# Performer attention and a channel mixer on one core: batch 2's DRAM copies moved ahead of the channel weights, the second weights moved behind its transposes, tails of q and k loaded as fp16, k evacuated by ScalarE

## The chip, the cores and the metric

The kernel runs on one core of a Trainium2 chip. The metric is device microseconds of one execution. Engines are named as in the profile: PE (matrix multiplies; PEld its weight loads), DVE (VectorE), ACT (ScalarE), POOL (GpSimd) and SP (SyncE, here only a queue that issues DMAs).

## The reference

Eight batches of eight heads, 576 positions, head size 64. Attention with random features, then a mixer over tokens and channels:

```
proj = x @ omega.T ; phi(x) = exp(proj - |x|^2/2 - max) / sqrt(128)      # x = q or k, scaled by 64 ** -0.25
kv   = phi(k).T @ v ; z = sum(phi(k)) ; x = (phi(q) @ kv) / (phi(q) @ z + 1e-6)
x    = heads side by side: [8, 576, 512]
u    = x + (relu(x.T @ w_tok1) @ w_tok2).T          # tokens: 576 -> 256 -> 576
out  = u + relu(u @ w_ch1) @ w_ch2                  # channels: 512 -> 1536 -> 512
```

Factors that are common to a row of q cancel in the division, so the kernel needs only exponentials of the projections and a maximum for k.

## The kernel before, in words

Each sequence of 576 is split into a main part of 512 and a tail of 64. For each batch the kernel needs q and k with the head size on the partitions (`qT`, `kT`), since the projection with `omega` contracts over it. There are two ways to them.

Batches 0 and 1 (the start): main parts are loaded through the GpSimd software DMA queue, which casts to fp16 on the way (`load_nat`), and PE transposes them (`t_main`, L255) into PSUM; DVE copies the result out (L258). The first two heads of batch 0 come as fp32 through SP's and ACT's queues and are cast by DVE (`stage_qk`, `cast_qk`). Tails come as fp32 through SP's and ACT's queues (`stage_tail`, L131), are cast by DVE (L265), transposed by PE (L268) and copied out by DVE (L269).

Batches 2 to 7: `cast_dram` (L80) copies q and k as fp16 into DRAM through the software queue, and `load_T` (L88) loads them with DMA transposes issued on SP's queue. The main part and the tail lie together in that copy. `load_T_v` also issues the loads of v (L106) and of v's tail (L115) on SP, behind the transposes.

Per batch, then: `q_tail` (L278) and `k_tail` (L289: a copy of k's tail columns; L293) project the tails; for each pair of heads `q_proj` (L327) and `k_proj` (L339) with exponentials on ACT (L272); `k_max` takes k's maximum on DVE (L351, L355, L359) and multiplies v by its reciprocal (L360; on DVE for batch 0, on POOL after); `kv` (L372, L377) and ACT's copy (L385); `num` (L396), `norm` (L404, L405), `num_tail` (L418, L427, L428). The tail's maximum and multiplies are `k_tail_max` (L305 to L315). Token mixing is `tok1` (L441, L444), `tok2` (L457, L460) and a transpose on PE (L480, L481); channel mixing is `ch1` (L495, relu on ACT L502) and `ch2` (L507, add on DVE L516, store L518). `ch1` reads the first channel weights `wc1` (loaded in two halves, L228), `ch2` the second, `wc2` (two halves, L234); in the profile both are named `wc`.

The order on every engine is written by hand: each step gets a place, one unit per pair of heads (batch b begins at 4b), from a table of offsets (`L`, `O`, `O1`), and the steps are issued sorted by place. An engine works through its instructions in that order; a DMA on POOL or SP is one of them, so a DMA that has to wait holds what stands behind it. The software queue has eight completion slots in turn: a DMA on POOL also waits until the one issued eight before it has landed.

Of the kernel before, what the change touches and what calls it, by code (L numbers as in the profile page):

```python
# [9 lines left out]
FP32 = mybir.dt.float32  # L10
FP16 = mybir.dt.float16
# [6 lines left out]
def kernel(  # L18
# [17 lines left out]
    nc = tc.nc  # L36

    B, H, S, D = q.shape
# [5 lines left out]
    SM = 512  # L44
    ST = S - SM
# [8 lines left out]
    ldpool = ctx.enter_context(tc.tile_pool(name="ld", bufs=3))  # L54
# [7 lines left out]
    def att_ps(shape, dt, name):  # L62
        return pspool.tile(shape, dt, name=name, tag="attps", bufs=3)
# [8 lines left out]
    SP2 = S // 2  # L72
    NP2 = SM // 2
    live = {}
# [18 lines left out]
    def load_v(b):  # L93

        if b < 2:
            t = ldpool.tile([P, H, NJ, D], FP16, name="v_16", tag="v_16", bufs=2)
            live["v", b] = t
            nc.gpsimd.dma_start(
                out=t.rearrange("p h j d -> p h (j d)"),
                in_=v[b, :, 0:SM, :].rearrange("h (p j) d -> p h (j d)", j=NJ),  # L100
            )
# [18 lines left out]
    stage = {}  # L120
# [4 lines left out]
        eng.dma_start(out=t, in_=src[0, 0:2, 0:SM, :].rearrange("h (p j) d -> p h (j d)", j=NJ))  # L125
        stage[which] = t

    def stage_tail(eng, b, which):
        src = q if which == "q" else k
        t = ldpool.tile([ST // 2, H, 2 * D], FP32, name=f"stt_{which}", tag="stt", bufs=2)  # L130
        eng.dma_start(out=t, in_=src[b, :, SM:S, :].rearrange("h (c w) d -> c h (w d)", w=2))  # L131
        stage[which, b] = t

    def new_nat(b):
        for which in "qk":
# [20 lines left out]
    stage_qk(nc.scalar, "k")  # L156
    om_f = wpool.tile([P, D], FP32, name="om_f")
    nc.sync.dma_start(out=om_f, in_=omega)
    stage_tail(nc.scalar, 0, "k")
    stage_tail(nc.sync, 0, "q")  # L160
    ident16 = wpool.tile([P, P], FP16, name="ident16")
    make_identity(nc, ident16)
    load_nat(0, 2, 4, "q")
    load_nat(0, 2, 4, "k")
    load_nat(0, 4, 8, "q")
    load_nat(0, 4, 8, "k")
    load_v(0)
    load_v_tail(0)

# [14 lines left out]
    wc1 = wpool.tile([P, ND, DC], FP16, name="wc1")  # L184
    wc2 = wpool.tile([P, NCB, DM], FP16, name="wc2")
# [40 lines left out]
    def load_wc1(part):  # L226
        c0, c1 = part * DC // 2, (part + 1) * DC // 2
        nc.gpsimd.dma_start(  # L228
            out=wc1[:, :, c0:c1], in_=moe_w_ch1[:, c0:c1].rearrange("(i p) c -> p i c", p=P)
        )  # L230
# [11 lines left out]
    def at(place, fn, *args):  # L242
        steps.append((place, len(steps), fn, args))


    def t_main(b, h0, n, which):

        if h0 == 0:
            live[which + "T", b] = ldpool.tile(
                [P, H, SP2], FP16, name=f"{which}T", tag=f"{which}T", bufs=2  # L250
            )
        ps = att_ps([P, n, 2, P], FP16, "t_ps")
        for i in range(n):
            for e in range(2):
                nc.tensor.transpose(  # L255
                    ps[:, i, e, :], live[which + "nat", b][:, h0 + i, e * P : (e + 1) * P], ident16
                )
        nc.vector.tensor_copy(  # L258
            out=live[which + "T", b][:, h0 : h0 + n, 0:NP2],
            in_=ps.rearrange("r h e p -> r h (e p)"),  # L260
        )

    def t_tail(b, which):
        nt = ldpool.tile([ST // 2, H, 2 * D], FP16, name="natt", tag="natt", bufs=1)
        nc.vector.tensor_copy(out=nt, in_=stage[which, b])  # L265
        ps = att_ps([P, H, ST // 2], FP16, "tt_ps")
        for h in range(H):
            nc.tensor.transpose(ps[:, h, :], nt[:, h, :], ident16[0 : ST // 2, 0 : ST // 2])  # L268
        nc.vector.tensor_copy(out=live[which + "T", b][:, :, NP2:SP2], in_=ps)  # L269

    def exp(out, in_):
        nc.scalar.activation(out=out, in_=in_, func=AF.Exp, bias=0.0, scale=c_scale)  # L272
# [13 lines left out]
    def k_tail(b):  # L286
        sb = live["kT", b]
        kt = apool.tile([P, H, ST // 2], FP16, name="k_tt", tag="k_tt")
        nc.vector.tensor_copy(out=kt, in_=sb[:, :, NP2:SP2])  # L289
        live["kpt", b] = apool.tile([P, 4, M], FP16, name="k_pt", tag="k_pt")  # L290
        ps = att_ps([P, 4, M], FP32, "kt_ps")
        for g in range(2):
            nc.tensor.matmul(  # L293
                ps[:, 2 * g : 2 * g + 2, :],
                kt[:, 4 * g : 4 * g + 4, :].rearrange("r h c -> r (h c)"),
                bd,
                start=True,
                stop=True,
            )
        exp(live["kpt", b], ps)  # L300
# [222 lines left out]
            nc.sync.dma_start(out=out[2 * j + 1, SM:S, :], in_=o[ST:P])  # L523


    L = {"dram2": 2.516, "wc2": 2.862, "tq": -0.681, "tk": -0.669, "tail": 0.285, "dram": 2.006, "T": 2.8, "klo": 1.094, "khi": 3.57, "clo": 4.0}
    O = {"qt": -0.334, "kt": 0.536, "ktm": 1.279, "q0": 0.018, "q1": 0.449, "k0": 0.06, "k1": 0.182, "km": 0.711, "kv": 1.426, "num": 1.72, "dn": 0.204, "norm": 1.74, "nt": 2.248}
    O1 = {"qt": 2.914, "kt": 0.685, "ktm": 1.13}
    def load_second():
        load_wtok()  # L530
        load_nat(1, 0, 4, "q")
        load_nat(1, 0, 4, "k")
        load_nat(1, 4, 8, "q")
        load_nat(1, 4, 8, "k")
        load_v(1)
        stage_tail(nc.sync, 1, "q")
        stage_tail(nc.sync, 1, "k")
        load_v_tail(1)
        load_wc1(0)
        load_wc1(1)  # L540

    at(-0.97, cast_qk, "q")
    at(-0.96, cast_qk, "k")
    at(-0.90, load_second)
    at(L["dram2"], cast_dram, 2, "q")
    at(L["dram2"], cast_dram, 2, "k")
    at(L["wc2"], load_wc2, 0)
    at(L["wc2"], load_wc2, 1)
    at(0.05, clear_vz)
    at(0.95, clear)  # L550
    at(2.95, permute_w2)
    for b in range(2):
        n = 2 if b == 0 else 4
        for h0 in range(0, H, n):
            at(4 * b + h0 / 2 + L["tq"], t_main, b, h0, n, "q")
            at(4 * b + h0 / 2 + L["tk"], t_main, b, h0, n, "k")
        at(4 * b + L["tail"], t_tail, b, "k")
        at(4 * b + L["tail"] + 0.001, t_tail, b, "q")

    def load_T_v(b):  # L560
        for which in "qk":
# [8 lines left out]
        at(4 * (b - 2) + L["T"], load_T_v, b)  # L570

    for b in range(B):
        o = dict(O)
        if b < 2:
            o.update(O1)
# [24 lines left out]

    for b in range(B):
        items = [(5, tok1, b, 0), (5, tok1, b, 1), (2, tok2, b, 0), (2, tok2, b, 1)]
        items += [(1, tokT, b, 0), (2, tok2, b, 2), (1, tokT, b, 1), (2, tok2, b, 3)]
        if b % 2:
            items += [(4, tok2_tail, b // 2)]
        items += [(1, tokT, b, 2), (1, tokT, b, 3)]
        if b % 2:
            items += [(1, u_transpose, ut[b // 2], uTt[:, :, b // 2, :])]
        spread(4 * (b + 1) + L["klo"], 4 * (b + 1) + L["khi"], items)

    for c in range(B + 1):
        items = [(4, ch1, c, cb) for cb in range(NCB)] + [(12, ch2, c, j) for j in range(NJ)]
        spread(4 * (c + 1) + L["clo"], 4 * (c + 2) + L["clo"], items)

    for _, _, fn, args in sorted(steps, key=lambda s: s[:2]):
        fn(*args)
# [30 lines left out]
```

## Time and profile before

| | us |
|---|---|
| median of 3 runs | 339.85 (339.14 to 340.18) |
| the profiled execution | 338.85 |
| its span, first to last instruction | 336.8 |
| PE busy | 305.8 |
| DVE busy | 180.9 |
| ACT busy | 152.3 |
| POOL busy | 69.0 |

In the profile's rows a number behind an operation's `x` counts instructions; the figure in brackets is the engine's idle time just before the row and what ended it. A DMA's "us to landing" runs from its issue until its data are there. Durations come from the one profiled execution.

### The profile page before, as it was taken

How to read it: one execution, taken by the hardware profiler on the slowest of the kernel's cores; microseconds unless marked ns; L12 is line 12 of the kernel's file. 1: busy time of each engine (PE TensorE's matmuls, PEld its weight loads, DVE VectorE, ACT ScalarE, POOL GpSimd, SP SyncE). 2: the span in 40 equal slices, each digit the busy share in tenths (PEclk: the TensorE clock that was granted, in tenths of full speed). 3: DMA queues.
4: the chain of work that ended last, by engine and by line, in shares of the span. 5: the costliest groups of instructions: out<-in, count | busy, mean ns of one | idle time of the engine just before them, and what ended most of it. 6: DMA issues, size and time to landing. Idle time of an engine off the chain costs nothing.

```text
span 336.8 us, 5538 instructions
## 1 busy us (share of the span) xinstructions
PE 305.8 (91%) x2137; PEld 162.6 (48%) x2137; DVE 180.9 (54%) x479; ACT 152.3 (45%) x293; POOL 69.0 (20%) x92
## 2 busy tenths in 40 slices
PE   5666781699999999999999999999999999999994
PEld 2444540354555555555555555555555544444441
DVE  3898894254855386547754865576548415202011
ACT  1545360385248525842585267426742540250620
POOL 8540341024112411331132124012401100000000
PEclk9657798599999999999999999999999999999999
DMA  9999995998358537772767294001001001102014
GB/s 177 206 201 215 204 196 100 229 183 190 103 104 241 105 99 145 201 140 64 152 194 140 64 220 125 31 33 63 2 31 65 31 2 62 62 2 93 31 31 93
DMA packets 59689, 39.01 MB, mean 116 GB/s; under 512 B 30096, under 2 KB 54544, under 8 KB 59280
## 3 DMA queue, kind: packets, MB, share of 16 engines
q1 hardware_dynamic: 49552, 24.55, 30.1%
q0 software_dynamic: 9568, 13.73, 24.7%
q10 hardware_dynamic: 544, 0.39, 0.4%
q8 instruction: 16, 0.26, 0.3%
q14 instruction: 9, 0.07, 0.1%
HBM read 35.88 MB, written 16.52 MB: 156 GB/s over the span
## 4 chain that ended last, share of the span: by engine, by line
PE 74%; DMA 14%; POOL 4%; DVE 4%; SPq 3%; issue 1%; POOLq 0%
PE h_ps L507 28%; PE h_ps L495 25%; DMA q<-in_q_dram 6%; DMA kT<-k 5%; PE ht_ps L457 4%; PE k_ps L339 3%; DMA w2raw<-in_moe_w_tok_dram 3%; PE q_ps L327 3%; SPq L88 3%; POOL vz L315 2%; PE h_ps L441 2%; PE uT_ps L480 2%; PE num_ps L396 2%; PE kv_ps L372 1%; PE kv_ps L377 1%; PE htt_ps L468 1%
## 5 line engine op out<-in xcount | busy, mean ns | idle before, releaser
L507 PE MATMUL h_ps<-wc,r 128*128 128x512 f16 x432 | 98.1, 379 | 0.0
L495 PE MATMUL h_ps<-uT,wc 128*128 128x512 f16 x384 | 93.9, 382 | 0.0
L502 ACT ACTIVATE r<-h_ps 128x512 f16<-128x512 f32 x108 | 64.6, 598 | 57.7 <-PE h_ps L495 57.3
L507 PEld LDWEIGHTS <-r 128*128 128x128 f16 x432 | 41.1, 98 | 45.1
L272 ACT ACTIVATE q_p<-q_ps 128x512 f16<-128x512 f32 x64 | 38.3, 598 | 49.8 <-PE q_ps L327 49.7
L495 PEld LDWEIGHTS <-wc 128*128 128x128 f16 x432 | 41.0, 98 | 40.4 <-issue 0.8
L360 POOL TENSOR_TENSOR v_sc<-v_nat,v_sc 128x512 f16<-128x512 f32 x24 | 25.4, 1057 | 129.0 <-DVE rc L404 71.2
L516 DVE TENSOR_TENSOR o_sb<-um,h_ps 128x512 f32<-128x512 f16 x32 | 22.0, 688 | 50.7 <-PE h_ps L507 50.4
L272 ACT ACTIVATE k_p<-k_ps 128x512 f16<-128x512 f32 x64 | 36.5, 601 | 1.1 <-PE k_ps L339 1.1
L404 DVE RECIPROCAL rc<-num_ps 128x4 f32<-128x4 f32 x64 | 10.9, 171 | 32.8 <-PE num_ps L396 32.7
L385 ACT CAST kv_sb<-kv_ps 128x130 f16<-128x130 f32 x32 | 8.5, 267 | 44.2 <-PE kv_ps L377 44.2
L405 DVE TENSOR_TENSOR xm<-num_ps,rc 128x256 f16<-128x256 f32 x64 | 27.2, 424 | 2.2
L327 PE MATMUL q_ps<-qT,bd 128*128 128x512 f16 x64 | 26.2, 409 | 1.0 <-DVE qT L258 1.0
L339 PE MATMUL k_ps<-bd,kT 128*128 128x256 f16 x128 | 25.3, 296 | 0.9 <-DMA kT<-k 0.7
L315 POOL TENSOR_TENSOR vz<-v_tail,vz 32x256 f16<-32x256 f32 x28 | 18.6, 663 | 33.5 <-DVE vz L314 21.7
L460 DVE TENSOR_TENSOR um<-xm,ht_ps 128x512 f16<-128x512 f16 x32 | 21.9, 683 | 2.2 <-PE ht_ps L457 1.9
L355 DVE TENSOR_REDUCE km<-mx 128x8 f16<-128x512 f16 x32 | 22.0, 686 | 1.1
L396 PEld LDWEIGHTS <-q_p 128*128 128x128 f16 x256 | 16.6, 102 | 12.3 <-issue 1.8
L457 PE MATMUL ht_ps<-r,w2m 128*128 128x512 f16 x64 | 19.2, 379 | 0.9 <-DVE r L450 0.5
L339 PEld LDWEIGHTS <-kT 128*128 128x128 f16 x128 | 13.0, 105 | 12.3 <-issue 1.4
L351 DVE TENSOR_TENSOR mx<-k_p 128x512 f16<-128x512 f16 x32 | 13.9, 434 | 9.3 <-ACT k_p L272 9.1
L396 PE MATMUL num_ps<-kv_sb,q_p 128*128 128x65 f16 x256 | 18.4, 200 | 0.6 <-ACT kv_sb L385 0.3
(92 smaller groups left out, 278.7 us busy)
## 6 DMA issues: line engine op xcount, KB each, us to landing
out_dram<-o_sb SPq DMA_DIRECT2D x32, 256.0 KB, 2.4
v_nat<-in_v_dram SPq DMA_DIRECT2D x12, 512.0 KB, 5.4
q<-in_q_dram POOLq DMA_DIRECT2D x6, 576.0 KB, 5.5
k<-in_k_dram POOLq DMA_DIRECT2D x6, 576.0 KB, 8.8
wc<-in_moe_w_ch_dram POOLq DMA_DIRECT2D x4, 768.0 KB, 19.9
v_tail<-in_v_dram SPq DMA_DIRECT2D x32, 32.0 KB, 4.9
v<-in_v_dram POOLq DMA_DIRECT2D x2, 512.0 KB, 10.4
out_dram<-o_sb SPq DMA_DIRECT2D x8, 128.0 KB, 2.3
```

The costliest lines, as they stand in the source:

```text
L272: nc.scalar.activation(out=out, in_=in_, func=AF.Exp, bias=0.0, scale=c_scale)
L315: eng.tensor_tensor(out=vs[r, hh, :, 0:D], in0=live["vt", b][r], in1=vs[r, hh, :, D : D + 1].broadcast_to((32, 4, D)), op=ALU.mult,)
L327: nc.tensor.matmul(ps, bd[:, w * M : (w + 1) * M], sb[:, 2 * hp : 2 * hp + 2, 0:NP2], start=True, stop=True)
L339: nc.tensor.matmul(ps[:, 2 * e : 2 * e + 2, :], sb[:, 2 * hp + i, e * P : (e + 1) * P], bd, start=True, stop=True,)
L355: nc.vector.reduce_max(out=mx, in_=tmp, axis=AX.X)
L360: eng.tensor_tensor(out=vs[:, :, 0:D], in0=live["v", b][:, 2 * hp : 2 * hp + 2].rearrange("p h j d -> p (h j) d"), in1=vs[:, :, D : D + 1] ...
L396: nc.tensor.matmul(ps[:, j, :], live["qp", b, hp][:, j % 2, i, j // 2, :], sb, start=True, stop=True)
L405: nc.vector.tensor_tensor(out=live["x", b][:, :, h * D : (h + 1) * D], in0=ps[:, :, 0:D], in1=rc.unsqueeze(2).broadcast_to((P, NJ, D)), op ...
L457: nc.tensor.matmul(ps, w2m[:, tb, j, :], live["r1", b][:, tb, :], start=(tb == 0), stop=(tb == NT - 1))
L495: nc.tensor.matmul(ps, wc1[:, db, cb * P : (cb + 1) * P], uT[:, db].rearrange("p j c -> p (j c)"), start=(db == 0), stop=(db == ND - 1),)
L502: nc.scalar.activation(out=live["r3", c][:, cb, :], in_=ps, func=AF.Relu)
L507: nc.tensor.matmul(ps, live["r3", c][:, cb, j * P : (j + 1) * P], wc2[:, cb, :], start=(cb == 0), stop=(cb == NCB - 1),)
```

## The change

Six edits.

1. `cast_dram` of batch 2 gets place 1.8 (2.516 before), and the loads of the first channel weights, which stood at the end of `load_second` (place -0.90), get place 1.85, behind it.
2. The loads of the second channel weights, place 2.862 before, stand at 8.473, directly behind `k_tail` of batch 2.
3. The tails of q and k of batches 0 and 1 are loaded as fp16 through the software queue (`load_nat_tail`, L131), in three buffers. The casts on DVE and the loads on SP and ACT go.
4. In `t_main`, k's result leaves PSUM through ACT, q's still through DVE (one line, L258 to L259).
5. The copy in `k_tail` goes to POOL from batch 2 on.
6. The table: batches 0 and 1 get tables of their own, in which a few projections move; from batch 2 on k's projections stand later (0.06 to 0.207 and 0.182 to 0.468), `k_tail` earlier (0.536 to 0.472), token mixing earlier (1.094 to 1.017), and the copies into DRAM of batches 3 to 7 later (2.006 to 2.766).

```diff
-    def stage_tail(eng, b, which):
+    def load_nat_tail(b, which):
         src = q if which == "q" else k
-        t = ldpool.tile([ST // 2, H, 2 * D], FP32, name=f"stt_{which}", tag="stt", bufs=2)
-        eng.dma_start(out=t, in_=src[b, :, SM:S, :].rearrange("h (c w) d -> c h (w d)", w=2))
-        stage[which, b] = t
+        t = ldpool.tile([ST // 2, H, 2 * D], FP16, name="natt", tag="natt", bufs=3)
+        nc.gpsimd.dma_start(out=t, in_=src[b, :, SM:S, :].rearrange("h (c w) d -> c h (w d)", w=2))
+        live[which + "natt", b] = t
...
-        nc.vector.tensor_copy(
+        copy = nc.vector.tensor_copy if which == "q" else nc.scalar.copy
+        copy(
             out=live[which + "T", b][:, h0 : h0 + n, 0:NP2],
...
-        nt = ldpool.tile([ST // 2, H, 2 * D], FP16, name="natt", tag="natt", bufs=1)
-        nc.vector.tensor_copy(out=nt, in_=stage[which, b])
+        nt = live[which + "natt", b]
...
-        nc.vector.tensor_copy(out=kt, in_=sb[:, :, NP2:SP2])
+        (nc.vector if b < 2 else nc.gpsimd).tensor_copy(out=kt, in_=sb[:, :, NP2:SP2])
...
-    at(L["wc2"], load_wc2, 0)
-    at(L["wc2"], load_wc2, 1)
+    at(L["wc1"], load_wc1, 0)
+    at(L["wc1"], load_wc1, 1)
+    for part in range(2):
+        at(8 + O["kt"] + L["wc2"], load_wc2, part)
```

What this does to the order on POOL between batch 1's loads and the second weights, before (`q_374` and `k_376` are batch 2's copies in DRAM, `q_698` and `k_700` batch 3's, `wc_129` the first and `wc_130` the second channel weights, `v_sc` the multiplies of batch 1's v):

```order
L98 DMA v_155<-in_v_dram 128x8x256
L228 DMA wc_129<-in_moe_w_ch_dram 128x4x768 x2
L80 DMA q_374<-in_q_dram 32x9216
L80 DMA k_376<-in_k_dram 32x9216
L234 DMA wc_130<-in_moe_w_ch_dram 128x6x512 x2
L360 TENSOR_TENSOR v_sc<-v_155,v_sc 128x8x64
L315 TENSOR_TENSOR vz_139<-v_tail,vz_139 32x4x64 x4
L360 TENSOR_TENSOR v_sc<-v_155,v_sc 128x8x64
L80 DMA q_698<-in_q_dram 32x9216
L80 DMA k_700<-in_k_dram 32x9216
L360 TENSOR_TENSOR v_sc<-v_155,v_sc 128x8x64 x2
```

And now, at the same place (`q_324` and `k_326` batch 2's, `q_752` and `k_754` batch 3's copies; `natt` a tail of batch 1):

```order
L131 DMA natt<-in_k_dram 32x8x128
L131 DMA natt<-in_q_dram 32x8x128
L98 DMA v_159<-in_v_dram 128x8x256
L80 DMA q_324<-in_q_dram 32x9216
L80 DMA k_326<-in_k_dram 32x9216
L228 DMA wc_129<-in_moe_w_ch_dram 128x4x768 x2
...
L80 DMA q_752<-in_q_dram 32x9216
L80 DMA k_754<-in_k_dram 32x9216
L360 TENSOR_TENSOR v_sc<-v_159,v_sc 128x8x64
L289 COPY k_tt<-kT 128x256
L234 DMA wc_130<-in_moe_w_ch_dram 128x6x512 x2
```

Batch 2's copies have passed the first weights; the second weights stand behind batch 1's last multiply and behind the copy of k's tail columns, which reads the transposed k of batch 2. Batch 3's copies stand behind one more multiply than before.

On DVE, the end of batch 1's first pair of heads and the tails of batch 1, as a difference:

```order
-L265 CAST natt<-stt_k 32x1024
 L269 COPY kT<-tt_ps 128x8x32
-L265 CAST natt<-stt_q 32x1024
 L269 COPY qT<-tt_ps 128x8x32
 L289 COPY k_tt<-kT 128x256
```

Both casts are gone, and the two copies out of PSUM follow each other.

More of the change, by code (lines that the diff above doesn't have):

```diff
@@ L158 @@
     nc.sync.dma_start(out=om_f, in_=omega)
-    stage_tail(nc.scalar, 0, "k")
-    stage_tail(nc.sync, 0, "q")
     ident16 = wpool.tile([P, P], FP16, name="ident16")
@@ L166 @@
     load_nat(0, 4, 8, "k")
+    load_nat_tail(0, "k")
+    load_nat_tail(0, "q")
     load_v(0)
@@ L523, in ch2 @@
             nc.sync.dma_start(out=out[2 * j + 1, SM:S, :], in_=o[ST:P])
-    L = {"dram2": 2.516, "wc2": 2.862, "tq": -0.681, "tk": -0.669, "tail": 0.285, "dram": 2.006, "T": 2.8, "klo": 1.094, "khi": 3.57, "clo": 4.0}
-    O = {"qt": -0.334, "kt": 0.536, "ktm": 1.279, "q0": 0.018, "q1": 0.449, "k0": 0.06, "k1": 0.182, "km": 0.711, "kv": 1.426, "num": 1.72, "dn": 0.204, "norm": 1.74, "nt": 2.248}
-    O1 = {"qt": 2.914, "kt": 0.685, "ktm": 1.13}
+    L = {"dram2": 1.8, "wc2": 0.001, "dram": 2.766, "T": 2.8, "klo": 1.017, "khi": 3.57, "clo": 4.0, "klo0": 1.094, "khi0": 3.57, "clo0": 4.0, "wc1": 1.85}
+    O = {"qt": -0.334, "kt": 0.472, "ktm": 1.279, "q0": 0.018, "q1": 0.449, "k0": 0.207, "k1": 0.468, "km": 0.711, "kv": 1.426, "num": 1.72, "dn": 0.204, "norm": 1.74, "nt": 2.248}
+    O0 = {"qt": 2.914, "kt": 0.685, "ktm": 1.13, "q0": 0.018, "q1": 0.525, "k0": -0.372, "k1": 0.182, "km": 0.711, "kv": 1.426, "num": 1.72, "dn": 0.204, "norm": 1.74, "nt": 2.248, "tq": -0.681, "tk": -0.669, "tail": 0.327}
+    O1 = {"qt": 2.914, "kt": 0.685, "ktm": 1.13, "q0": -0.375, "q1": 0.613, "k0": 0.06, "k1": 0.182, "km": 0.711, "kv": 1.426, "num": 1.72, "dn": 0.219, "norm": 1.74, "nt": 2.248, "tq": -0.681, "tk": -0.669, "tail": 0.285}
     def load_second():
@@ L534, in load_second @@
         load_nat(1, 4, 8, "k")
+        load_nat_tail(1, "k")
+        load_nat_tail(1, "q")
         load_v(1)
-        stage_tail(nc.sync, 1, "q")
-        stage_tail(nc.sync, 1, "k")
         load_v_tail(1)
-        load_wc1(0)
-        load_wc1(1)
     at(-0.97, cast_qk, "q")
@@ L553 @@
         n = 2 if b == 0 else 4
+        o = (O0, O1)[b]
         for h0 in range(0, H, n):
[L555 to L558, printed above, removed]
+            at(4 * b + h0 / 2 + o["tq"], t_main, b, h0, n, "q")
+            at(4 * b + h0 / 2 + o["tk"], t_main, b, h0, n, "k")
+        at(4 * b + o["tail"], t_tail, b, "k")
+        at(4 * b + o["tail"] + 0.001, t_tail, b, "q")
     def load_T_v(b):
@@ L572 @@
     for b in range(B):
-        o = dict(O)
-        if b < 2:
-            o.update(O1)
+        o = (O0, O1)[b] if b < 2 else O
         g = 4 * b
@@ L608 @@
             items += [(1, u_transpose, ut[b // 2], uTt[:, :, b // 2, :])]
-        spread(4 * (b + 1) + L["klo"], 4 * (b + 1) + L["khi"], items)
+        klo, khi = (L["klo0"], L["khi0"]) if b == 0 else (L["klo"], L["khi"])
+        spread(4 * (b + 1) + klo, 4 * (b + 1) + khi, items)
     for c in range(B + 1):
         items = [(4, ch1, c, cb) for cb in range(NCB)] + [(12, ch2, c, j) for j in range(NJ)]
-        spread(4 * (c + 1) + L["clo"], 4 * (c + 2) + L["clo"], items)
+        spread(4 * (c + 1) + L["clo0" if c == 0 else "clo"], 4 * (c + 2) + L["clo"], items)
     for _, _, fn, args in sorted(steps, key=lambda s: s[:2]):
```

## The prediction

> **What bounds the kernel now.** I read the page first, then busy time by stage (windows cut where the matmul stream changes character), then the timeline at the hole this shows, then the queues behind the hole. From the page the clock granted to TensorE in 40 slices, and the stages (start:end, length, then busy us and instruction count of PE, PEld, DVE, ACT, POOL, the clock, DMA share, GB/s):
>
> ```profile
> PEclk9657798599999999999999999999999999999999
> ...
> 8.00:26.80 18.80, 13.35 (x106) 8.23 (x106) 16.66 (x50) 9.41 (x19) 8.88 (x12) 0.60 1.36 203
> 26.80:52.30 25.50, 19.02 (x205) 12.68 (x203) 22.53 (x64) 12.18 (x26) 6.86 (x9) 0.90 1.25 191
> 52.30:61.20 8.90, 0.00 (x0) 0.00 (x0) 2.27 (x6) 0.09 (x1) 1.05 (x1) 0.71 0.77 117
> ...
> 81.90:300.00 218.10, 216.86 (x1537) 115.28 (x1535) 122.03 (x315) 107.21 (x209) 39.45 (x48) 1.00 0.40 98
> ```
>
> Three regimes. From 81.9 to 300 us PE is busy 216.86 of 218.10 us: this stretch can't shrink by more than about 1 us, it can only start earlier. From 8 to 52.3 us DVE is the fullest engine (16.66 of 18.8, 22.53 of 25.5) while PE has holes. From 52.3 to 61.2 us PE does nothing. The timeline says why (start, length, engine, line; in brackets the idle time before it and what ended it):
>
> ```profile
> 51.86 0.40 PE L480 MATMUL uT_ps<-ident,um 128*128 128x128 f16 x4
> 61.23 0.61 PE L278 MATMUL qt_ps<-qT,bd 128*128 128x256 f16 x2 [8.97 <-DMA qT<-q]
> ...
> 68.39 0.38 PE L293 MATMUL kt_ps<-bd,k_tt 128*128 128x256 f16 x2
> ...
> 81.86 1.46 PE L507 MATMUL h_ps<-wc,r 128*128 128x512 f16 x6
> ```
>
> Batch 2's first matmul waits 8.97 us for the DMA transpose of its q. GpSimd's timeline shows in which order the software queue was fed, and single answers on DMA issues give each landing after its issue:
>
> ```profile
> 14.57 0.89 POOL L98 DMA_DIRECT2D v<-in_v_dram  x1 [0.52 <-DMA w1m<-in_moe_w_tok_dram]
> 16.69 1.50 POOL L228 DMA_DIRECT2D wc<-in_moe_w_ch_dram  x2 [1.23 <-DMA w2raw<-in_moe_w_tok_dram]
> 18.17 0.54 POOL L80 DMA_DIRECT2D q<-in_q_dram  x1
> 19.29 0.51 POOL L80 DMA_DIRECT2D k<-in_k_dram  x1 [0.58 <-DMA q_nat<-in_q_dram]
> 20.64 0.87 POOL L234 DMA_DIRECT2D wc<-in_moe_w_ch_dram  x1 [0.84 <-DMA k_nat<-in_k_dram]
> 21.97 0.83 POOL L234 DMA_DIRECT2D wc<-in_moe_w_ch_dram  x1 [0.46 <-DMA q_nat<-in_q_dram]
> 46.09 0.52 POOL L80 DMA_DIRECT2D k<-in_k_dram  x1
> 49.06 1.05 POOL L360 TENSOR_TENSOR v_sc<-v,v_sc 128x512 f16<-128x512 f16 x1 [2.45 <-PE k_ps L339]
> 54.92 1.05 POOL L360 TENSOR_TENSOR v_sc<-v,v_sc 128x512 f16<-128x512 f16 x1 [4.81 <-DVE v_sc L359]
> ```
> ```profile
> v<-in_v_dram POOLq DMA_DIRECT2D x1, 512.0 KB, 12.3
> wc<-in_moe_w_ch_dram POOLq DMA_DIRECT2D x1, 768.0 KB, 16.6
> q<-in_q_dram POOLq DMA_DIRECT2D x1, 576.0 KB, 18.6
> k<-in_k_dram POOLq DMA_DIRECT2D x1, 576.0 KB, 20.2
> wc<-in_moe_w_ch_dram POOLq DMA_DIRECT2D x1, 768.0 KB, 27.7
> k<-in_k_dram POOLq DMA_DIRECT2D x1, 576.0 KB, 15.2
> ```
>
> Issue plus landing: batch 1's v at 26.9, the second half of the first weights at 34.0 (issued half way through the pair, 17.4), q's copy at 36.8, k's at 39.5, the second weights at 49.7, batch 3's copies at 61.3. They land in the order of issue, one after the other. The transposes start only when q's copy is there, and SP's DMA queue shows how long they take beside the rest, against batch 4's:
>
> ```profile
> 36.80 9.21 SPq L88 DMA_TRANSPOSE qT<-q  x1
> ...
> 95.05 2.44 SPq L88 DMA_TRANSPOSE qT<-q  x1
> 97.58 3.16 SPq L88 DMA_TRANSPOSE kT<-k  x1
> ```
> ```profile
> 46.11 17.22 DMA kT<-k
> ```
> ```profile
> kT<-k SPq DMA_TRANSPOSE x1, 6.8
> ```
>
> Batch 2's pair takes from 36.8 to 63.3, 26.5 us; batch 4's, with the queue empty, from 95.05 to 104.4, 9.3 us.
>
> **The change, part by part.**
>
> *Copies ahead of the first weights.* The two weight loads stood for 34.0 - 26.9 = 7.1 us in front of q's copy. The four fp16 tails (64 KB each) join the same queue: at the weights' own rate (2 x 768 KB in 7.1 us) 1.2 us. So q's copy lands at 36.8 - 7.1 + 1.2 = 30.9. For the transposes, the work that shared the engines before was: rest of k's copy 2.7, second weights 10.2, batch 3's copies 11.6, transposes 9.3; 33.8 us of work done in 26.5, a ratio of 0.78. Now: 2.7 + 7.1 (first weights, now behind) + 9.3 = 19.1, times 0.78 is 14.9, so kT lands at about 45.8. The ends are 30.9 + 9.3 = 40.2 (undisturbed) and 30.9 + 26.5 = 57.4 (as slow as before). I take 45.8, because batch 3's copies, which came last before, are issued behind one more GpSimd multiply, the one at 49.06; 4 us earlier (next step) that one ends at 46.1, after the transposes.
>
> *When PE gets there.* DVE sets the pace before the hole, so what leaves DVE counts. The DVE groups between 8 and 52 us, two casts' aftermath, and the first max of batch 0:
>
> ```profile
> L258 DVE COPY kT<-t_ps 128x512 f16<-128x512 f16 x4 | 1.7, 417 | 0.0
> L258 DVE COPY kT<-t_ps 128x1024 f16<-128x1024 f16 x2 | 1.4, 677 | 0.0
> L265 DVE CAST natt<-stt_q 32x1024 f16<-32x1024 f32 x2 | 1.3, 672 | 0.0
> L265 DVE CAST natt<-stt_k 32x1024 f16<-32x1024 f32 x2 | 1.3, 644 | 0.0
> ```
> ```profile
> 13.29 0.42 DVE L351 TENSOR_TENSOR mx<-k_p 128x512 f16<-128x512 f16 x1
> ...
> 34.87 0.29 DVE L269 COPY kT<-tt_ps 128x256 f16<-128x256 f16 x1 [0.45 <-PE tt_ps L268]
> 36.23 0.29 DVE L269 COPY qT<-tt_ps 128x256 f16<-128x256 f16 x1 [0.49 <-PE tt_ps L268]
> ```
>
> 5.7 us of DVE work go away. In batch 1: two k copies 1.36, two casts 1.32, and the round trips 0.45 + 0.49 in which DVE waited for PE between them; 3.6 us. In batch 0 the tails now come through the software queue, fifth and sixth in it; DVE then waits for them in order instead of casting, so the casts and the first two k copies buy nothing there, as the first max comes at about 13.3 either way; the other two k copies give 0.8. Together 4.4; I take 4.0, since PE is at 0.60 of its clock in batch 0 and close behind. Ends: 1.5 (tails land late) and 5.7. ScalarE takes the k copies beside 12.18 of 25.5 busy us, at no cost; were it full, each would cost about the 0.42 or 0.68 us that it took on DVE. The Trainium skill, "DMA: Bandwidth & Descriptors", Specifications, speaks against this part: under 512 B per transfer the engines read, modify and write, and the fp16 tail rows are 256 B. By it (an estimate, at double price) the tails take 2.4 us instead of 1.2, batch 0 starts 1.2 us later and the result is 326.2; no run before shows such rows in this queue.
>
> PE then reaches batch 2 at 52.3 - 4.0 = 48.3, after kT (45.8). The wait of 9.0 us goes and the arrival moves by 4.0.
>
> *The clock.* Behind the hole the clock was low:
>
> ```profile
> 61.20:66.50 5.30, 4.60 (x21) 2.27 (x22) 1.35 (x5) 2.56 (x5) 0.00 (x0) 0.52 1.09 278
> ```
>
> 5.3 us at 0.52 would be 2.8 at full clock: 2.5 us saved if no hole is left. The Trainium skill, "TensorE: Matmul & The Clock Gate", Part 1, has the clock back after about 3.4 us of work; by it 1.7 us would be saved and the time would be 325.8. Here it stayed low for 5.3 us, so I keep 2.5.
>
> *Second weights held.* They stand behind the new copy of k's tail on GpSimd, which waits for kT; queued behind it are the weights and the multiplies for batch 2. The last multiply of batch 1 moves from 54.92 to 50.9 and ends at 52.0; the copy takes at most such a multiply's 1.05, I take 0.5; kt's matmul wants it at 48.3 + (68.39 - 61.23) - 2.5 = 53.0, so nothing is lost there. The first half is issued at 52.5 and takes 0.87 us to issue (row at 20.64), so the second stands at 53.4. The first use, L507, comes 81.86 - 61.23 - 2.5 = 18.1 us after PE's arrival, at 66.4. The shortest landing of such a half is this row's, the longest the 27.7 above:
>
> ```profile
> wc<-in_moe_w_ch_dram POOLq DMA_DIRECT2D x1, 768.0 KB, 13.6
> ```
>
> That gives 67.0 to 81.1, a wait of 0.6 to 14.7 us (0 if it is quicker). I take 0.6: the 27.7 had four transfers in front of it, now only what is left of batch 3's copies.
>
> *The rest.* The fourth tail buffer waits until PE has transposed batch 0's k tail; v, both copies and the weights queue behind it, but PE should be done with it at about 13 (the max at 13.3 stands behind it on DVE), and GpSimd comes there at about 14 (v's issue in the row at 14.57). DVE loses the six later tail copies; it isn't the bound after 61 us. k's projections stand later among the channel matmuls from batch 2 on; with 1.2 us of PE idle in 218, I put this at 0, within 1 us either way.
>
> **The sum**: 9.0 + 4.0 + 2.5 - 0.6 = 14.9. The profiled execution took 338.85 us (span 336.8), so 323.95; the median of the runs shown, 339.85, is 1.0 higher: 325.0.
>
> **The rivals.**
>
> *The transposes still collide.* If the first weights and batch 3's copies hold them back as before, PE waits until 57.4: 9.1 us and the clock's 2.5 come back, 3.3 remain, 336.6. For it: 26.5 against 9.3 us in the rows. Against: one competitor less. By the Trainium skill, "DMA: Bandwidth & Descriptors", Queues, rings and completion order, each DMA engine alternates between queues by packet, so that transposes beside weights crawl until these are through; that speaks for it.
>
> *Second weights late, transposes in time.* A landing half way between 13.6 and 27.7 is 7 us later: 332.
>
> *Slower.* Place: L507 behind the copy of k's tail. If kT lands at 57.4, the second half is issued at 57.4 + 0.5 + 0.87 = 58.8 and at 27.7 lands at 86.5, while PE wants it at 57.4 + 20.6 = 78.0: 8.5 us of wait against 3.9 gained (the collision's 3.3 and the 0.6 counted there), 344.5. It decides from a landing of 23 us on. Against: what fills the queue now stands in front, not behind.
>
> *Nothing of it*: GpSimd already waits for old transfers before each issue, so an earlier place need not land earlier; then 339.85. Against: landing follows issue order in every row.
>
> **Chances.** Forecast 0.66, collision 0.14, late weights 0.12, slower 0.05, nothing 0.03. About 0.3% can be told from no change here. So faster 0.92, same 0.03, slower 0.05. The forecast's own range is 322 to 329 (start gain 1.5 to 5.7, reordering 1). For 8 in 10 it reaches to 333, which takes in the late weights and the milder collisions, and down to 320.5.
>
> **What would show it.** Right: q's copy landing near 31, kT near 46, no DMA wait before PE's third L278 pair near 48, clock 1.0 there, L507 first near 67. Wrong: a wait for qT or kT of over 2 us, tails that hold batch 0 past 14 us, or L507 waiting for wc.

## The result, and the profile after

| | us | ratio to before |
|---|---|---|
| before, median of 4 runs beside it | 340.01 (339.14 to 342.24) | |
| changed kernel, median of 4 runs | 320.73 (320.09 to 321.38) | 0.9424 [0.9373, 0.9474] |
| its profiled execution | 321.38 | |
| its span | 318.9 (before 336.8) | |

The kernel became 19 us faster; the forecast was 325.0. Times and ratios of the experiments below leave disturbed runs out, and the profiles of two of them (the casts back on DVE, the clearing first) fell into such runs and are not read.

The page's row of granted clocks, in 40 slices, no longer has the gap behind the start:

```profile
PEclk9598999999999999999999999999999999999998
```

The stages of the changed kernel (start:end, length, then busy us and count of PE, PEld, DVE, ACT, POOL, the clock, DMA share, GB/s):

```profile
8.00:26.80 18.80, 12.26 (x115) 7.94 (x116) 14.62 (x45) 11.60 (x23) 8.79 (x14) 0.73 1.42 202
26.80:47.00 20.20, 16.11 (x197) 10.32 (x195) 19.05 (x59) 13.07 (x27) 6.72 (x9) 1.00 1.11 207
47.00:52.30 5.30, 5.13 (x44) 2.95 (x42) 3.30 (x10) 4.54 (x10) 2.62 (x4) 1.00 1.16 255
...
65.00:280.00 215.00, 214.44 (x1528) 114.50 (x1527) 120.53 (x310) 105.72 (x207) 41.22 (x55) 1.00 0.49 110
```

Batch 1 is over at 47.0 and not at 52.3, at full clock where it had 0.90; PE then goes on without a pause. DVE is still the fullest engine up to there (19.05 of 20.2 us), as it was before. PE's timeline at the place where the hole was, and at the first use of the second weights:

```profile
46.62 0.40 PE L480 MATMUL uT_ps<-ident,um 128*128 128x128 f16 x4 [0.32 <-DVE um L460]
47.07 0.38 PE L278 MATMUL qt_ps<-qT,bd 128*128 128x256 f16 x2
65.19 2.75 PE L507 MATMUL h_ps<-wc,r 128*128 128x512 f16 x12
```

No bracket stands behind L278 or L507: neither waits. SP's queue, and DMA issues with their time to landing:

```profile
29.69 8.44 SPq L88 DMA_TRANSPOSE qT<-q  x1
38.23 4.94 SPq L88 DMA_TRANSPOSE kT<-k  x1
```
```profile
q<-in_q_dram POOLq DMA_DIRECT2D x1, 576.0 KB, 10.2
kT<-k SPq DMA_TRANSPOSE x1, 7.0
wc<-in_moe_w_ch_dram POOLq DMA_DIRECT2D x1, 768.0 KB, 9.8
wc<-in_moe_w_ch_dram POOLq DMA_DIRECT2D x1, 768.0 KB, 13.9
wc<-in_moe_w_ch_dram POOLq DMA_DIRECT2D x2, 768.0 KB, 11.9
```

GpSimd's queue shows when the second weights are issued:

```profile
50.69 0.39 POOL L289 COPY k_tt<-kT 128x256 f16<-128x256 f16 x1
51.02 1.75 POOL L234 DMA_DIRECT2D wc<-in_moe_w_ch_dram  x2
```

kT has landed at 38.23 + 7.0 = 45.2, 1.9 us before PE wants batch 2. The first half of the second weights lands at 51.02 + 9.8 = 60.8. The second, issued at about 51.9, takes 13.9 and lands at 65.8 (the last row is the mean of the two); the seventh of L507's twelve matmuls, at about 65.19 + 6 x 0.22 = 66.5, is the first that reads it. That is a margin of 0.7 us.

### The profile page after: what moved, and what is told of

It is laid out like the page before. It is cut to its first block, busy times and chain, and to the rows that moved or that the text cites. A ratio compares the mean times of both kernels' runs of the same rounds, so it can differ in the third digit from the quotient of the medians.

```text
span 318.9 us, 5525 instructions
## 1 busy us (share of the span) xinstructions
PE 299.3 (94%) x2137; PEld 159.1 (50%) x2137; DVE 173.8 (55%) x463; ACT 155.8 (49%) x299; POOL 71.6 (22%) x102
## 4 chain that ended last, share of the span: by engine, by line
PE 81%; DVE 10%; DMA 3%; POOL 3%; issue 1%; ACT 0%; POOLq 0%; DVEq 0%
PE h_ps L507 29%; PE h_ps L495 28%; PE ht_ps L457 4%; PE k_ps L339 3%; PE q_ps L327 3%; PE h_ps L441 3%; DMA v<-in_v_dram 3%; PE uT_ps L480 2%; PE num_ps L396 2%; PE kv_ps L372 2%; DVE xm L405 1%; PE kv_ps L377 1%; DVE km L355 1%; PE htt_ps L468 1%; POOL vz L315 1%
## 5 line engine op out<-in xcount | busy, mean ns | idle before, releaser
L507 PE MATMUL h_ps<-wc,r 128*128 128x512 f16 x432 | 98.1, 379 | 0.0
L507 PEld LDWEIGHTS <-r 128*128 128x128 f16 x432 | 41.0, 98 | 45.8
L516 DVE TENSOR_TENSOR o_sb<-um,h_ps 128x512 f32<-128x512 f16 x32 | 22.0, 688 | 48.0 <-PE h_ps L507 47.6
L272 ACT ACTIVATE k_p<-k_ps 128x512 f16<-128x512 f32 x64 | 37.8, 598 | 2.8 <-PE k_ps L339 1.5
L351 DVE TENSOR_TENSOR mx<-k_p 128x512 f16<-128x512 f16 x32 | 13.6, 425 | 37.0 <-ACT k_p L272 37.0
L327 PE MATMUL q_ps<-qT,bd 128*128 128x512 f16 x64 | 24.9, 395 | 1.6 <-DVE qT L259 1.6
L315 POOL TENSOR_TENSOR vz<-v_tail,vz 32x256 f16<-32x256 f32 x28 | 17.3, 616 | 17.0 <-DVE vz L314 15.4
L396 PE MATMUL num_ps<-kv_sb,q_p 128*128 128x65 f16 x256 | 17.9, 195 | 0.1
L339 PEld LDWEIGHTS <-kT 128*128 128x128 f16 x128 | 12.1, 100 | 10.6 <-ACT kT L259 1.7
L441 PE MATMUL h_ps<-xm,w1m 128*128 128x512 f16 x64 | 16.4, 379 | 0.0
## 6 DMA issues: line engine op xcount, KB each, us to landing
wc<-in_moe_w_ch_dram POOLq DMA_DIRECT2D x4, 768.0 KB, 14.9
```

What stands on the lines that cost most here:

```text
L327: nc.tensor.matmul(ps, bd[:, w * M : (w + 1) * M], sb[:, 2 * hp : 2 * hp + 2, 0:NP2], start=True, stop=True)
L339: nc.tensor.matmul(ps[:, 2 * e : 2 * e + 2, :], sb[:, 2 * hp + i, e * P : (e + 1) * P], bd, start=True, stop=True,)
L396: nc.tensor.matmul(ps[:, j, :], live["qp", b, hp][:, j % 2, i, j // 2, :], sb, start=True, stop=True)
L441: nc.tensor.matmul(ps, w1m[:, j, tb * P : (tb + 1) * P], live["x", b][:, j, :], start=(j == 0), stop=False)
L507: nc.tensor.matmul(ps, live["r3", c][:, cb, j * P : (j + 1) * P], wc2[:, cb, :], start=(cb == 0), stop=(cb == NCB - 1),)
```

## The experiments

Twelve kernels ran, in three groups. The theories: that the place of batch 2's copies in the queue made the hole go, as the prediction's working had it; or that it is the traffic behind them, whatever their place. The start's 5.2 us and the 1.2 us gained later have terms of their own. The letters in the expectations change their meaning: in the first group A and B are what each expectation says of them (in the second of its runs B, not A, is the view that the place alone made the hole go); in the second group B is the view that the place decides and C that the traffic does.

### The place of batch 2's copies, alone and undone

The kernel before, with nothing but batch 2's copies ahead of the first weights:

```diff
-        load_wc1(0)
-        load_wc1(1)
...
-    L = {"dram2": 2.516, ...
+    L = {"dram2": 1.8, ...
+    at(1.85, load_wc1, 0)
+    at(1.85, load_wc1, 1)
```

> The kernel before with one edit alone: batch 2's copies ahead of the first weights; the second weights follow directly, and all else is as before. Theory A: q's copy lands at about 29.7 instead of 36.8, but first and second weights (17.3 us of queue) and then batch 3's copies (issued at 45.5) run beside the transposes; with the ratio of 0.78 kT lands at about 52.6, when PE comes (52.3): the 9 us hole and 2.5 us of clock go, 328 to 330 us. Rival B (what stands behind the copies slows the transposes as much as what stood in front): kT lands at 58 to 62 and the time stays at 336 to 340 us.

Measured: 337.74 (335.98 to 339.38, 10 runs), ratio 0.9938 [0.9908, 0.9968]. SP's queue, the landing of its second transpose, and PE at batch 2:

```profile
29.82 10.40 SPq L88 DMA_TRANSPOSE qT<-q  x1
40.32 21.52 SPq L88 DMA_TRANSPOSE kT<-k  x1
```
```profile
kT<-k SPq DMA_TRANSPOSE x1, 23.6
```
```profile
62.07 0.61 PE L278 MATMUL qt_ps<-qT,bd 128*128 128x256 f16 x2 [9.57 <-DMA qT<-q]
```

The transposes start at 29.8, 7 us earlier than before, and kT lands at 40.32 + 23.6 = 63.9, where it landed before (63.3). Going first brings kT no earlier when the first weights, the second and batch 3's copies come behind; where the 0.6% of time comes from was not taken apart. Rival B came, with a landing 1.9 us beyond its range. The other way round, the changed kernel with the first weights ahead of the copies again:

```diff
-"wc1": 1.85}
+"wc1": 1.75}
```

> The changed kernel with one edit taken back: the first channel weights are issued ahead of batch 2's copies again; the second weights stay held. Theory A (the queue lands in order, and only the order of issue matters): q's copy lands 7 to 10 us later than the changed kernel's 29.7, at 37 to 39.5, kT 9.3 to 12 us after that, at 46 to 51, and PE, which is ready at 47.1, waits 0 to 4 us: 321 to 325 us. Rival B (this order alone removed the 9 us hole): the hole comes back, 330 us or more, with the clock low behind it.

Measured: 320.02 (319.83 to 321.16, 4 runs), ratio 0.9434 [0.9398, 0.9469], the changed kernel's own time.

```profile
36.89 3.91 SPq L88 DMA_TRANSPOSE qT<-q  x1
40.96 2.40 SPq L88 DMA_TRANSPOSE kT<-k  x1
```
```profile
kT<-k SPq DMA_TRANSPOSE x1, 4.6
```

The pair starts 7 us later and is through at 40.96 + 4.6 = 45.6, 0.4 us after the changed kernel's: with nothing but k's copy beside it, it takes 8.7 us instead of 15.5.

### The second weights, alone and undone

The kernel before, with the second weights held back and nothing else:

```diff
-    at(L["wc2"], load_wc2, 0)
-    at(L["wc2"], load_wc2, 1)
+    at(8 + O["kt"] + 0.001, load_wc2, 0)
+    at(8 + O["kt"] + 0.001, load_wc2, 1)
```

> The kernel before, with one part of edit 2 alone: both loads of the second weights stand at place 8.537, behind batch 2's k_tail, instead of 2.862; the order of the first weights and of batch 2's copies stays as before. Theory C (it is the traffic behind batch 2's copies, not their place, that slows the transposes): q's copy still lands at about 37, but with nothing but k's copy and batch 3's copies in the queue the pair of transposes takes 9 to 14 us instead of 26.5, so that kT lands at 46 to 51, ahead of PE's arrival at 52.3; the wait of 9.0 us and the 2.5 us of low clock go, 11.5 us gained, about 328.5, or up to 3 us more if the second weights come late. Theory B (the place of batch 2's copies decides, as the prediction had it): transposes that cannot start before 37 still collide with batch 3's copies, the wait stays over 4 us and the gain is under 5 us, over 335.

Measured: 326.67 (326.09 to 326.75, 5 runs), ratio 0.9672 [0.9593, 0.975]. The runs of the kernel before beside this kernel, the next two and the one with the late places undone spread from 334.57 to 351.09 us, so that these four ratios are on record as unclear; what follows goes by the traces and by the distance to the changed kernel's time.

```profile
36.80 2.94 SPq L88 DMA_TRANSPOSE qT<-q  x1
39.84 3.21 SPq L88 DMA_TRANSPOSE kT<-k  x1
```
```profile
kT<-k SPq DMA_TRANSPOSE x1, 5.2
```
```profile
51.79 0.38 PE L278 MATMUL qt_ps<-qT,bd 128*128 128x256 f16 x2
```

The transposes start at the same 36.80 as before, the pair takes 8.2 us instead of 26.5, and PE comes to batch 2 at 51.79 without a wait. The span falls from 336.8 to 324.8: 61.23 - 51.79 = 9.4 us of arrival and 2.6 of clock behind it. That is two thirds of the changed kernel's 17.9, with batch 2's copies at their old place. Now the changed kernel with the second weights directly behind the first:

```diff
-        at(8 + O["kt"] + L["wc2"], load_wc2, part)
+        at(1.86, load_wc2, part)
```

> The changed kernel, with the loads of the second weights at place 1.86, directly behind the first weights, so that they are in the queue while batch 2's transposes run. Theory C: the transposes stretch again from 15.6 us to 20 to 30 us, kT lands at 52 to 62, PE waits 5 to 15 us for it and the time is 328 to 338. Theory B: q's copy still lands at 30, the pair gets through as in the changed kernel within 3 us, no wait of over 1 us, 320 to 323.

Measured: 336.31 (335.62 to 338.85, 9 runs), ratio 0.9946 [0.9897, 0.9996].

```profile
29.45 11.35 SPq L88 DMA_TRANSPOSE qT<-q  x1
40.91 20.58 SPq L88 DMA_TRANSPOSE kT<-k  x1
```
```profile
kT<-k SPq DMA_TRANSPOSE x1, 22.6
```
```profile
61.64 0.61 PE L278 MATMUL qt_ps<-qT,bd 128*128 128x256 f16 x2 [15.02 <-DMA qT<-q]
```

With that one line the hole is back, longer than before (15.02 us against 8.97), since PE arrives earlier. It costs 15.6 of the 19 us; the view that the place of the copies decides has fallen.

### Batch 3's copies

The changed kernel, with the copies of batches 3 to 7 at their old place:

```diff
-"dram": 2.766,
+"dram": 2.006,
```

> The changed kernel, with the copies of batches 3 to 7 in DRAM at their old place (2.006 instead of 2.766), so that batch 3's are issued at about 40 instead of about 47, while batch 2's transposes still run. If batch 3's copies count as the second weights do: kT lands 4 to 10 us later than 45.2, PE waits 2 to 8 us, 323 to 331. If not (they only meet the last third of the transposes): under 1.5 us, 320 to 322.

Measured: 320.63 (320.10 to 320.89, 4 runs), ratio 0.9496 [0.9403, 0.9589]; the changed kernel's time. POOL's issue of batch 3's q and SP's of batch 2's kT:

```profile
40.40 0.57 POOL L80 DMA_DIRECT2D q<-in_q_dram  x1
```
```profile
37.77 4.93 SPq L88 DMA_TRANSPOSE kT<-k  x1
```

At 40.40 half of the second transpose has been issued, so the copies meet the end of the pair. The time hides that they count: kT lands 9.8 us after its issue, at 47.6, 2.4 us later than in the changed kernel, and PE's first matmul on k of batch 2 comes only at 49.1. The two halves of batch 2's v, issued at 42.8 and 43.4, behind these copies, take 9.1 and 11.0 us; in the changed kernel, where the copies follow v, 4.3 and 5.3. What the copies would do to transposes in mid-course this run does not say.

### The terms of the start

The tails as fp32 with casts on DVE, as before:

```diff
-        nt = live[which + "natt", b]
+        nt = ldpool.tile([ST // 2, H, 2 * D], FP16, name="natt", tag="natt", bufs=1)
+        nc.vector.tensor_copy(out=nt, in_=stage[which, b])
...
```

The loads go back to SP's and ACT's queues with it.

> The changed kernel with the tails of batches 0 and 1 loaded as fp32 on SP's and ACT's queues and cast by DVE, as before. Theory A (DVE paces the start, and the hole that its casts made in batch 1 also cost PE its clock): PE reaches batch 2 about 2.3 us (casts and round trips) plus up to 1.7 us (3.4 us at half clock) later than 47.1, at 49.4 to 51, and the time is 323 to 325 us; a low clock shows around 34 to 38. Rival B (the earlier arrival comes from the queue, that is from batch 1's data landing earlier): no cost, 320 to 321.5 us.

Measured: 323.68, 324.05, 324.64 and 324.87, ratio 0.9553 [0.9518, 0.9588]: about 3.6 us above the changed kernel. Then k out of PSUM through DVE again:

```diff
-        copy = nc.vector.tensor_copy if which == "q" else nc.scalar.copy
+        copy = nc.vector.tensor_copy
```

> The changed kernel with k's transposes of batches 0 and 1 copied out of PSUM by DVE again. Theory A (DVE paces the start): 1.36 us in batch 1 and 0.8 to 1.6 in batch 0 come back, PE reaches batch 2 at about 49.3 to 50, and the time is 322.5 to 324 us. Rival B (ScalarE's copies take 0.6 us against 0.42 and are on PE's path, so they gave nothing): 320 to 321.5 us.

Measured: 322.08, 322.29 and 323.31, ratio 0.9501 [0.946, 0.9543]: about 1.6 us above. PE's arrival at batch 2 here:

```profile
49.16 0.38 PE L278 MATMUL qt_ps<-qT,bd 128*128 128x256 f16 x2
```

It is 2.1 us later than in the changed kernel. Both kinds of DVE work counted; the casts brought more than their own 2.6 us on DVE, k's copies less than their 3.1. The changed kernel did not run beside these two; where it ran again, it took 320.88 and not 320.73.

### The late places

The changed kernel, with the places of k's projections, k's tail and token mixing from batch 2 on as before:

```diff
-"klo": 1.017,  ... "kt": 0.472, ... "k0": 0.207, "k1": 0.468,
+"klo": 1.094,  ... "kt": 0.536, ... "k0": 0.06, "k1": 0.182,
```

> The changed kernel, with the places of edit 6 from batch 2 on undone (k's projections, k's tail and token mixing where they stood). The prediction put these at 0 within 1 us; the traces show 1.2 us less from the first L507 to the end. If the places are the cause: 321.5 to 322.5. If it is something else that goes with the start: within 0.5 us of the changed kernel, 320.3 to 321.2.

Measured: 322.45 (322.06 to 323.88, 6 runs), 1.7 us above the changed kernel. PE's timeline:

```profile
47.52 0.38 PE L278 MATMUL qt_ps<-qT,bd 128*128 128x256 f16 x2
65.44 1.78 PE L507 MATMUL h_ps<-wc,r 128*128 128x512 f16 x7
```

Its span is 320.7: from the first L507 to the end 255.3 us against 318.9 - 65.19 = 253.7. The places are worth 1.6 us in that stretch, and are the cause of the 1.2 us seen there; the kernel with only the second weights held, which has the old places, needs 254.9 us from its first L507 (69.88) to the end, as the kernel before does. The stage from 65 to 280 us shows some of it:

```profile
65.00:280.00 215.00, 213.77 (x1522) 113.98 (x1521) 121.52 (x311) 105.07 (x206) 42.14 (x55) 1.00 0.47 111
```

PE is busy 0.7 us less here than in the changed kernel (213.77 against 214.44); the rest is no idle time of PE, and was not taken apart.

### What bounds the start next

The third group asks whether the start can be shortened further, with the changed kernel run again beside it:

> The changed kernel itself, without an edit, as the measure for the three beside it: 320 to 321.5 by every theory.

Measured: 320.88 (320.16 to 321.56, 5 runs). First, DVE's clearing of four buffers ahead of batch 0's work:

```diff
-    at(0.95, clear)
+    at(-1.5, clear)
```

> The changed kernel, with the clearing of four buffers (DVE L203 to L207, 0.9 us at 15.56) ahead of the work on batch 0, where DVE idles 3.5 us for omega. If DVE alone sets the pace up to batch 2, as the prediction had it: PE comes 0.8 us earlier to batch 2 and the time is 0.5 to 0.9 less than the changed kernel's. If PE or a transfer sets the pace as well: under 0.3 us.

Measured: 320.35, 320.39, 320.64, 323.71 and 324.55: three runs 0.2 to 0.5 us below the control's median, within the control's own spread, and two 3 to 4 above it. So no gain is shown, and the 0.5 to 0.9 expected of DVE alone did not come. Then besides that the tails and v of batch 0 earlier in the software queue:

```diff
-    load_nat(0, 4, 8, "q")
-    load_nat(0, 4, 8, "k")
     load_nat_tail(0, "k")
     load_nat_tail(0, "q")
     load_v(0)
+    load_nat(0, 4, 8, "q")
+    load_nat(0, 4, 8, "k")
```

> The kernel with the clearing first, and besides batch 0's tails and v ahead of the last four heads of its q and k in the software queue. DVE waits 1.72 us for the tails at 12.22 and 0.51 us for v at 14.86 in the changed kernel. If these waits go: 2 to 2.5 us less in all, PE at batch 2 at about 44.6, 318 to 318.8. But kT lands at 45.2 and the second weights at 65.8 by the same queue, so PE may then wait for one or both of them: 319 to 321, or a second cluster 5 to 12 us higher where the second weights come late.

Measured: 325.07 (322.21 to 326.88, 6 runs), 4.2 us above the control, from a start that is 1.1 us shorter. PE comes to batch 2 at 45.92 and not at 44.6, so half of the expected 2 to 2.5 us came. GpSimd's and PE's timelines, the answer on the tile of batch 2's v, and last the control's DMA issues of that tile:

```profile
58.91 1.05 POOL L360 TENSOR_TENSOR v_sc<-v_nat,v_sc 128x512 f16<-128x512 f32 x1 [7.28 <-DMA v_nat<-in_v_dram]
```
```profile
45.92 0.38 PE L278 MATMUL qt_ps<-qT,bd 128*128 128x256 f16 x2
...
60.02 0.40 PE L372 MATMUL kv_ps<-v_sc,k_p 128*128 128x65 f16 x8 [2.04 <-POOL v_sc L360]
61.29 0.36 PE L377 MATMUL kv_ps<-vz,k_pt 128*128 128x130 f16 x2 [0.87 <-POOL vz L315]
...
68.71 2.75 PE L507 MATMUL h_ps<-wc,r 128*128 128x512 f16 x12
```
```profile
DMA to landing us min/median/max: 4.3/9.6/14.8
```
```profile
v_nat<-in_v_dram SPq DMA_DIRECT2D x2, 512.0 KB, 4.8
```

One half of batch 2's v takes 14.8 us to land, where the control's two take 4.3 and 5.3. Batch 3's copies on POOL, and v on SP's queue, in this kernel and then in the control:

```profile
43.66 0.57 POOL L80 DMA_DIRECT2D q<-in_q_dram  x1
```
```profile
43.28 1.20 SPq L106 DMA_DIRECT2D v_nat<-in_v_dram  x2
```
```profile
44.75 0.57 POOL L80 DMA_DIRECT2D q<-in_q_dram  x1
```
```profile
43.55 1.20 SPq L106 DMA_DIRECT2D v_nat<-in_v_dram  x2
```

GpSimd comes to the copies 1.1 us sooner, while the second half of v is being issued; in the control they come at the end of that. That copies issued ahead of v slow it agrees with the kernel that had batch 3's copies early (9.1 and 11.0 us). The waits expected were for kT or the second weights; what came was a wait for v, which no expectation had named. The last of the group moves the copies of batches 3 to 7 and their transposes behind the second weights (`T` is batch 2's place too; SP issues its transposes at 31.34 here):

```diff
-"dram": 2.766, "T": 2.8,
+"dram": 4.48, "T": 4.5,
```

> As the one before, with the copies of batches 3 to 7 and their transposes later (4.48 and 4.5 instead of 2.766 and 2.8), so that the second weights pass batch 3's copies in the queue. If those copies are what makes the second weights late: these land 8 to 10 us after their issue and 5 us earlier, no wait at L507, and the time is that of the one before or up to 1 us less, without a higher cluster. If batch 3's transposes now come too late: a wait for qT ahead of batch 3, 1 to 5 us more.

Measured: 319.58 (319.46 to 319.59, 5 runs), ratio 0.9406 [0.9395, 0.9418]; the control's is 0.9445 [0.9431, 0.9459].

```profile
wc<-in_moe_w_ch_dram POOLq DMA_DIRECT2D x2, 768.0 KB, 9.1
```
```profile
45.93 0.38 PE L278 MATMUL qt_ps<-qT,bd 128*128 128x256 f16 x2
...
64.04 2.75 PE L507 MATMUL h_ps<-wc,r 128*128 128x512 f16 x12
```

The waits for v are gone, the second weights land 9.1 us after their issue, in the mean of both halves, instead of 11.9, the 1.1 us of the shorter start reach the end, and five runs lie within 0.13 us. It beats the control by 1.3 us (0.4%). Copies and transposes moved together, so what either did is not told apart.

## Why the prediction was right or wrong

The hole, its cause in the DMA transposes, the clock behind it and the absence of a new wait were forecast and came. One step failed in its mechanism: the 9.0 us at the hole were put down to the place of batch 2's copies, and it is the second weights held back that bring them (held alone, they close the hole; not held, it is back with the copies in their new place). And three terms of the sum were too small: PE's arrival (4.0, measured 5.2), the wait for the second weights (-0.6, measured 0) and the rest, put at 0 (measured 1.2). With the step from span to median they put the measured 320.73 below the forecast's own 322 to 329. In the order of the prediction's steps, as spans:

| step | forecast | measured |
|---|---|---|
| the wait at batch 2 goes | 9.0 | 9.0 |
| PE arrives earlier | 4.0 | 5.2 (52.3 to 47.07) |
| low clock behind the hole | 2.5 | 2.5 |
| wait for the second weights | -0.6 | 0 |
| the rest | 0 | 1.2 |
| sum | 14.9 | 17.9 = 336.8 - 318.9 |

**Copies ahead of the first weights.** The times were right (q's copy at 29.7 for 30.9, kT at 45.2 for 45.8; tails at the double price that the prediction weighed would have made q's copy later, not earlier), the name of the step was not. The working itself held the answer: it took all work that shares the engines, times 0.78. In that sum the first weights only change sides, from ahead of the copy to behind it, while the second weights and batch 3's copies drop out of it. The rule is fitted to the first of these runs and tested by the other five, each from the issue of qT to the landing of kT:

| kernel | work beside the pair | 0.78 x the sum | measured | kT lands |
|---|---|---|---|---|
| before | k's copy, second weights, copies 3 | (fitted) | 26.5 | 63.3 |
| copies first, alone | all of these and the first weights | 31.9 | 34.1 | 63.9 |
| changed, second weights not held | the same | 31.9 | 34.1 | 63.5 |
| changed | k's copy, first weights | 14.9 | 15.5 | 45.2 |
| changed, first weights ahead | k's copy | 9.4 | 8.7 | 45.6 |
| before, second weights held | k's copy | 9.4 | 8.2 | 45.0 |

The rule holds within 2.2 us. Going 7 us earlier past the first weights is paid back by sharing with them: 45.2 against 45.6. What counts is what is queued behind: with the second weights there kT lands at 63 to 64, without them at 45, in either order of the rest. Where they are held, batch 3's copies come when the transposes are all but through; where not, they come in while these still run and stretch them further. How the delay divides between the two was not isolated. In the three kernels with the hole the second weights have landed at 49.7, 56.5 and 58.1, the last of batch 3's copies at 61.3, 61.9 and 61.6, and kT follows 2.0 us behind these each time, closer than the rule; a pair that is through only when the queue beside it is empty fits as well (in the other three kernels kT follows 3.5 to 5.5 us behind the queue's last landing). Whether holding back batch 3's copies alone would have closed the hole was not run; by the rule (an estimate, 0.78 x 22.2 = 17.3 us for the kernel before without them) kT would land at 54.1, against PE's 52.3. The Trainium skill, "DMA: Bandwidth & Descriptors", Queues, rings and completion order, has each DMA engine take turns between the queues by packet. That the queues share is what the runs show (8.2 us for a pair nearly alone, 34.1 beside the software queue); how the turns are weighted they do not show.

**When PE gets there.** The step failed on size: it counted DVE's time and no clock. The prediction's windows show a clock of 0.90 in batch 1; part of that is left over from batch 0 (0.75 from 26.4 to 31.0 us), and the larger part follows a hole in batch 1 like the later one (the wait in before, then the clock behind it, before and after):

```profile
34.47 0.36 PE L268 MATMUL tt_ps<-ident,natt 32*128 32x32 f16 x8 [3.11 <-DVE natt L265]
```
```profile
35.00:39.50 4.50, 3.70 (x40) 2.75 (x41) 3.73 (x13) 2.07 (x5) 1.06 (x1) 0.62 1.03 201
```
```profile
35.00:39.50 4.50, 3.70 (x36) 2.01 (x33) 4.17 (x14) 2.76 (x5) 2.77 (x5) 1.00 1.30 198
```

PE waited for the casts, and the clock was below full behind it. With the casts gone, batch 1 runs at 1.00. The runs put the casts at 3.6 us and k's copies at 1.6 (2.1 by PE's arrival), 5.2 together. That this is just the arrival's 5.2 may be chance: each was taken back alone, the new tables of batches 0 and 1 never, and that the clock is what the casts cost beyond DVE's time is argued, since the one run with the casts back has no undisturbed profile. ACT took 0.59 and 1.01 us for k's copies where DVE took 0.42 and 0.68; it had room for them. That batch 0 gains little was right: the tails by the software queue make PE wait there, and batch 1's first transposes come only half a microsecond earlier than before (the last two rows, before and after).

```profile
11.79 0.80 PE L268 MATMUL tt_ps<-ident,natt 32*128 32x32 f16 x16 [1.75 <-DMA natt<-in_k_dram]
```
```profile
26.87 1.04 PE L255 MATMUL t_ps<-ident,q_nat 128*128 128x128 f16 x8
```
```profile
26.39 0.61 PE L255 MATMUL t_ps<-ident,q_nat 128*128 128x128 f16 x8
```

**The clock.** 2.5 us, as forecast from the 5.3 us at 0.52: from L278 to L507 PE needs 65.19 - 47.07 = 18.12 us, where it needed 81.86 - 61.23 = 20.63. That the size came out is partly luck: the two kernels in which the hole is back need 19.82 (copies first, alone) and 19.13 us (second weights not held) for the same stretch, only 1.7 and 1.0 more than the changed kernel, though their holes are longer. In the kernel with the shorter start, two waits of 2.04 and 0.87 us were enough for a low clock:

```profile
60.00:65.40 5.40, 4.52 (x26) 2.29 (x26) 1.33 (x3) 1.95 (x4) 2.93 (x5) 0.68 1.07 166
```

The Trainium skill, "TensorE: Matmul & The Clock Gate", Part 1, lets the clock fall after an idle window of about 3.4 us and has it back after as long; here no wait was longer than 2.04 us, and the clock came down all the same, to 0.50 from 62 to 64 us and back to 1.00 from 65, which is about as long as the Trainium skill says. The measurement decides: shorter waits cost clock too. That kernel reaches L507 4.7 us after the one with the late copies (68.71 against 64.04), 2.9 by waiting and 1.8 by the clock.

**Second weights held.** The landing was forecast as 13.6 for either half and the need at the first matmul of L507. In fact the first half takes 9.8, and the second is read only six matmuls later; no wait is left, with a margin of 0.7 us. The copy on POOL took 0.39 us for the 0.5 assumed.

**The rest** was put at 0 within 1 us, by the 1.2 us of PE idle in 218. The late places bring 1.6 us, more than the 1.2 of PE idle that was taken as the bound: a busy PE was not PE at its shortest.

**The median.** The forecast added 1.0 us, by which the median of before lay above its profiled execution. The changed kernel's profiled execution lies 0.65 us above its median; that alone is 1.65 of the 4.3 us by which 325.0 was too high, and the three terms above are 3.0, less 0.4 by which the profiled time fell less than the span.

**The rivals.** The collision is real: it is what happens with the second weights not held (336.31, where that rival said 336.6; so close by chance, since PE waits 15.0 us there and not 9.1), and holding them is what prevents it. The late second weights didn't come, by 0.7 us. That nothing would happen fell with the first landing, though of the reordering by itself little came (337.74).

## What to carry to other kernels

Before moving a transfer forward in a queue, add up what will run beside it until it is through: a DMA transpose is delayed by what is issued behind it as much as by what stands ahead, and holding back a large load that nobody needs yet can be worth more than any place in the order. When the hole closes, look at the margins of the next arrivals: here a start 1.1 us shorter made the kernel 4 us slower, until the next copies were moved back as well. Count a removed wait with the clock behind it.

## What was not expected of the hardware

A pair of DMA transposes of 576 KB each took 8.2 us with little beside it and 34.1 us with four halves of weights and batch 3's copies (4 x 768 and 2 x 576 KB) in the software queue beside it. Of the two halves of a batch's v (512 KB each) on SP's queue one took 4.3 and the other 14.8 us, where batch 3's copies were issued 1.1 us sooner than in the control, whose halves took 4.3 and 5.3. And TensorE's granted clock fell after waits of 2.04 and 0.87 us with 0.40 us of work between them, to a mean of 0.68 from 60.0 to 65.4 us.
